# Four layers on one core: other queues, buffers and orders where two layers meet

## The chip, the core and the metric

The kernel runs on one core of a Trainium2 chip. The metric is the device time of one execution in microseconds (us). The kernel before took 2582.68 us in the median of 3 runs (2582.19 to 2583.7).

A core has engines that run beside each other, each with its own list of instructions, worked off in order: TensorE (PE; its weight loads are shown as PEld), VectorE (DVE), ScalarE (ACT), GpSimd (POOL) and SyncE (SP), which here only issues DMAs. An instruction that waits for a semaphore holds up everything behind it on its engine.

## The reference, cut to what matters

Two kinds of layer follow each other, A, B, A, B, each with a layer norm before it and a residual around it. x is 2048 x 640, both kinds have 32 heads. A has heads of 20 and four segments of 512 tokens; B has heads of 128, 64 segments of 32 tokens, and 8 memory rows that each segment passes on to the next.

```python
def _A_ref(x, wq, wk, wv, wo, beta):           # Dh = 20, N = 4, L = 512
    ...
    for s in range(N):
        qs, ks, vs = (q[:, :, s].copy(), k[:, :, s].copy(), v[:, :, s].copy())
        p = _softmax(jnp.einsum('bhqd,bhkd->bhqk', qs, ks) * scale + mask, axis=-1)
        a_dot = jnp.einsum('bhqk,bhkd->bhqd', p, vs)
        pq = phi(qs)
        num = jnp.einsum('bhld,bhde->bhle', pq, M)
        den = jnp.einsum('bhld,bhd->bhl', pq, z)[..., None] + 1e-06
        outs.append(g * num / den + (1.0 - g) * a_dot)
        pk = phi(ks)
        M = M + jnp.einsum('bhld,bhle->bhde', pk, vs)
        z = z + jnp.einsum('bhld->bhd', pk)
    return concat(outs) @ wo

def _B_ref(x, mem0, Wq, Wk, Wv, Wo, seg_len):  # Dh = 128, 64 segments of 32, M = 8
    ...
    mem = mem0
    for s in range(n_seg):
        h = jnp.concatenate([mem, xs], axis=1)  # 40 rows
        q, k, v = (jnp.einsum('btd,dhe->bhte', h, W) for W in (Wq, Wk, Wv))
        p = _softmax(where(mask, jnp.einsum('bhqe,bhke->bhqk', q, k) * scale, -1e9))
        o = jnp.einsum('bhte,hed->btd', jnp.einsum('bhqk,bhke->bhqe', p, v), Wo)
        mem = o[:, :M, :].copy()
        outs.append(o[:, M:, :])
    return jnp.concatenate(outs, axis=1)

x = x + _A_ref(_layernorm(x), ...)
x = x + _B_ref(_layernorm(x), ...)
x = x + _A_ref(_layernorm(x), ...)
x = x + _B_ref(_layernorm(x), ...)
```

The memory rows of the last segment (the 8 rows of `mem` after s = 63) are not part of the output.

## The kernel before, in words

**Layer A** (line 251 on) works on a segment of four tiles of 128 tokens. `seg_norm` loads a tile (a_xt), takes its statistics on DVE (a_ln_st, a_ln_mv, a_ln_rstd) and makes the normed tile a_xn; `seg_tr` transposes it on PE (a_tps) and ACT or DVE copies it to a_xnT. `proj_q` and `proj_kv` make a_QP, a_KV and from them a_qT, a_KVt, a_kT. Then, for group after group, come scores (a_S), their exponentials (a_PT) and the rest. At the end of a segment `out_stage_b` (line 366 on) multiplies by wo (a_YP), adds the residual (a_xr, loaded here; line 372) on DVE to a_xnew, stores it (line 386), copies it to bf16 (a_xnb, line 389) and stores that as well (xres_bf, line 392). B's layer norm reads xres_bf. In the last segment the copy is ACT's. a_xnb is one buffer. `unread` (a_W) puts matmuls on PE whose result nobody reads.

**Layer B** (line 789 on) first does the things that have no recurrence: it loads b_wv (five chunks of 1 MB, line 776) and b_wo (eight chunks, line 780), norms the first rows (b_xt, b_lntps, b_HX, b_TX), and projects the last 8 tokens of 16 segments at a time: `tail_unit` (b_tail; 16 units of 20 matmuls: Q and K by 8 groups of heads), evacuated by `tail_evac` to b_tu (eight places, DVE and ACT by turns) and stored to b_QKd by SP (line 952). `vtail_unit` (b_vtail) does the same for V. Then come 64 steps. A step projects its 32 rows (8 of memory, 24 of the segment): Ka, Qa, Kb, Qb (halves of the heads, 20 matmuls each), transposes (b_TPak and so on), scores (b_SP), softmax, V (b_Va, b_Vb), P times V (b_OTP), copies to b_OTsb, output projection b_OPS with b_wo, and from that the next memory rows (b_msb, b_MT). The last 8 tokens of a segment are query rows one step later; so output rows come as 24 rows of one segment (b_XO, `store_head`) and 8 rows of the segment before. The latter are collected in b_OTdef over four steps and multiplied four steps later in chunks (`od_chunk`, b_OPSd, b_XOd, `tail_dma`). Step 63 is followed by nothing: the last collected rows (b_XOe) get a b_OPSd of their own behind it.

**What sets the order.** All PE instructions, and in layer B those of ACT, DVE and POOL too, are chained in the order of the program text (`_OrdNC`, line 120). Layer A's other engines are ordered by a key, `K.base` plus a lag for the kind of instruction. SP's DMAs are put in order by the tile scheduler. A DMA signals on one of eight semaphores in turn, and waits for the DMA eight before it. The pools of A and B lie over each other in SBUF: b_wv's 40 KB per partition cover the places of A's weights and of the pools pxT (a_xnT), pxt (a_xt) and pxn (a_xn). A tile waits for the last readers of what lay in its place (`reuse_waits="tile"`).

**A's weights** come padded: the first A layer stores a_wq_pad and a_wkv to DRAM, the second loads them from there in `load_A_weights` (lines 231 to 233), all by SP.

Of the kernel before, what the change touches and what calls it, by code (L numbers as in the profile page):

```python
# [28 lines left out]
D = 640  # L29
# [27 lines left out]
def build_consts(nc, tc, C):  # L57
    with ExitStack() as tctx:
        tp_ = tctx.enter_context(tc.tile_pool(name="consts_tmp", bufs=1))
        ones = tp_.tile([128, 128], F32, name="c_ones")  # L60
        nc.vector.memset(ones[:], 1.0)
        identf = tp_.tile([128, 128], F32, name="c_identf")
        nc.gpsimd.affine_select(out=identf[:], in_=ones[:], pattern=[[-1, 128]], compare_op=ALU.is_equal,
                                fill=0.0, base=0, channel_multiplier=1)
        nc.vector.tensor_copy(C.identb[:], identf[:])
        nc.vector.memset(C.mhalf[:], -0.5)
        negs = tp_.tile([128, 128], F32, name="c_negs")
        nc.vector.memset(negs[:], -1e9)
        neguf = tp_.tile([128, 128], F32, name="c_neguf")
        nc.gpsimd.affine_select(out=neguf[:], in_=negs[:], pattern=[[1, 128]], compare_op=ALU.is_gt,  # L70
                                fill=0.0, base=0, channel_multiplier=-1)
        for i in range(2):
            nc.vector.tensor_copy(C.negu[:, i, :], neguf[:])
        nc.vector.memset(C.pad[:], 0.0)
        nc.vector.memset(C.pad[:, 0, 0:2], 1.0)
        nc.vector.memset(C.pad[:, 1, 0:1], 1.0)
        nc.vector.memset(C.bdmask[:], 0.0)
        for j in range(4):
            nc.vector.memset(C.bdmask[32 * j:32 * j + 32, 32 * j:32 * j + 32], 1.0)
# [143 lines left out]

def load_A_weights(nc, W, A_wq, A_wk, A_wv, A_wo, padded, stage):

    first = not padded
    if first:
        for nm, src in (("wq", A_wq), ("wk", A_wk), ("wv", A_wv)):
            nc.sync.dma_start(stage[nm], src.rearrange("(c p) n -> p c n", p=128))
    else:  # L230
        nc.sync.dma_start(W.wq[:].rearrange("p c h s -> p (c h s)"), padded["wq"])
        nc.sync.dma_start(W.wkv[:].rearrange("p c g n -> p (c g n)"), padded["wkv"])
# [17 lines left out]
def layer_A(nc, tc, C, W, x_src, x_dst, src_is_bf16, nseg=4, out_bf16=False, xb_dst=None, load_w=None, side_loads=None):  # L250
# [7 lines left out]
    with ExitStack() as ctx:  # L258
# [69 lines left out]
        def seg_norm(n_, tt):  # L328
# [4 lines left out]
            for i in range(2):  # L333
                K("st").vector.bn_stats(out=stats[:, i, :], in_=xt[:, 320 * i:320 * i + 320])
            mv = sml.tile([128, nc.vector.BN_AGGR_DIM], F32, name="a_ln_mv", tag="ln_mv")
# [30 lines left out]
        def out_stage_b(n_, tt, halves=(0, 1)):  # L366
            d = SEG[n_]
            oT, xr = d["oT"][tt], d["xr"][tt]
            r0 = n_ * 512 + tt * 128
            if xr is None:  # L370
                xr = wkl.tile([128, D], BF16 if src_is_bf16 else F32, name="a_xr")
                nc.sync.dma_start(xr[:], x_src[r0:r0 + 128, :])
            if n_ == nseg - 1 and (tt or not src_is_bf16):
# [12 lines left out]
            nc.sync.dma_start(x_dst[r0:r0 + 128, :], xnew[:])  # L386
            xnb = w1l.tile([128, D], BF16, name="a_xnb")
            if n_ == nseg - 1:
# [227 lines left out]
        for tt in range(4):  # L616
            K.base = 0.1 * tt - 100.0
            seg_norm(0, tt)
            K.base = None
            unread((14 if src_is_bf16 else 6, 4, 4, 4)[tt])  # L620
            seg_tr(0, tt)
# [65 lines left out]
        def last_turns(c0, c1):  # L687
            d = SEG[nseg - 1]
            for tt in range(4):
                if c0 == 0:  # L690
                    if tt % 2 == 0:
                        d["tps"] = d.get("tps", []) + [psx.tile([128, 2, 2 * 512], BF16, name="a_otps", tag="x")]
                    xr = wkl.tile([128, D], BF16 if src_is_bf16 else F32, name="a_xr") if tt < 2 else None
                    if tt < 2:
                        nc.sync.dma_start(xr[:], x_src[512 * nseg - 512 + 128 * tt:512 * nseg - 384 + 128 * tt, :])
                    d["xr"][tt] = xr
                tps = d["tps"][tt // 2][:, tt % 2, 0:D].rearrange("p (c t) -> p c t", t=128)
                for c in range(c0, c1):
                    nc.tensor.transpose(tps[:, c, :], d["Onat"][:, tt, 128 * c:128 * c + 128], C.identb[:])
# [89 lines left out]
def layer_B(nc, tc, C, W, x_src, xb_src, x_dst, mem0, B_Wv, B_Wo, nsteps=64, out_bf16=False, tag=""):  # L789
# [8 lines left out]
    with ExitStack() as ctx:  # L798
# [252 lines left out]
        def x_out(ops_, XO_, store, nm):  # L1051
            nc.vector.tensor_tensor(out=XO_[:], in0=ops_[0:64, :], in1=XO_[:], op=ALU.add)
            if out_bf16:
                xo = wk.tile([64, 320], BF16, name=f"b_xnb{nm}", tag=f"xnb{nm}")
            else:
# [4 lines left out]
        def store_head(s):  # L1060
            def f(xo):
                for jj2 in range(2):
                    nc.sync.dma_start(d_half(x_dst[32 * s:32 * s + 24, :], jj2), xo[32 * jj2:32 * jj2 + 24, :].rearrange("t (c x) -> t c x", x=64))
            return f

        def tail_dma(s0, store, xo):
            x_ = x_dst if store else x_src
            for jj2 in range(2):
                sb = xo[32 * jj2:32 * jj2 + 32, :].rearrange("t (c x) -> t c x", x=64)
                dr = x_[32 * s0:32 * s0 + 128, :].rearrange("(i t) (c j x) -> i t j c x", t=32, j=2, x=64)[:, 24:32, jj2]  # L1070
                if store:
# [16 lines left out]

        def od_end():
            x_out(od["ps"], od["xo"], lambda xo: tail_dma(od["s0"], True, xo), "d")  # L1090
            od.clear()
# [8 lines left out]
        for s in range(nsteps):  # L1100
# [11 lines left out]
            for jj2 in range(2):  # L1112
                nc.sync.dma_start(XO[32 * jj2:32 * jj2 + 24, :].rearrange("t (c x) -> t c x", x=64), d_half(x_src[32 * s:32 * s + 24, :], jj2))

# [61 lines left out]
            ka = kq(Ka, "act")  # L1176
            Qa = thin_mm(cols, W.wq, 0, "b_Qa")
            qa = kq(Qa, "dve", SCB)
            Kb = thin_mm(cols, W.wk, 1, "b_Kb")
            kb = kq(Kb, "act")  # L1180
            Qb = thin_mm(cols, W.wq, 1, "b_Qb")
            qb = kq(Qb, "act", SCB)
# [4 lines left out]
            TPaq = transp4(qa, "b_TPaq")  # L1187
            scatter("dve", TPaq, 0, QT[s], 0, 8, 24)
            x_scatter(TPaq, 0, QT)
# [4 lines left out]
            TPbq = transp4(qb, "b_TPbq", po.tile([128, 4, 128], BF16, name="b_TPbq", tag="tail"))  # L1194
            scatter("dve", TPbq, 1, QT[s], 0, 8, 24)
            x_scatter(TPbq, 1, QT)
            SPb = mask_mm(1)
# [25 lines left out]
            if unit:  # L1223
                tail_evac(unit[0], unit[1], "act")
            otf = [ps_tile([128, 2, 4, 40] if j else [128, 4, 40], F32, "b_OTP") for j in range(4)]
            ots = {j: (otf[j][:, 0, :, :], otf[j][:, 1, :, :]) for j in (1, 2, 3)}
# [50 lines left out]
            if od and od["n"] == 4:  # L1277
                od_end()
                if last:
                    od_begin(s - 3, XOe, "tail")  # L1280
                else:
                    tail_dma(s - 3, False, XOd)
                    od_begin(s - 3, XOd)
            elif s == 3:
# [5 lines left out]
            x_out(ops, XO, store_head(s), "")  # L1290
            nc.gpsimd.tensor_copy(OTdef[(s // 4) % 2][:, :, 8 * (s % 4):8 * (s % 4) + 8], OTsb[:].rearrange("p (h c) -> p h c", c=40)[:, :, 0:8])
            if ln_due(s + 1):
                ln_load(ln_due(s + 1))
            QT.pop(s, None); KT.pop(s, None); VH.pop(s - 1, None)
        for _ in range(4):
            od_chunk()
        od_end()


def full_kernel(tc, A_x, A_wq, A_wk, A_wv, A_wo, A_beta, B_x, B_mem0, B_Wq, B_Wk, B_Wv, B_Wo, B_seg_len, out, layers="ABAB"):  # L1300
    nc = tc.nc
    with ExitStack() as ctx:
# [13 lines left out]
        for li, L in enumerate(layers):  # L1316
            lastl = (li == nl - 1)
            if L == "A":
                first = li == 0

                def side(slot, after):
                    if slot % 3 == 1 and slot // 3 < 8 * NCH:
                        load_B_resident(nc, WB, B_Wq, B_Wk, slot // 3, after)
                    if slot == 24:
                        keep_padded(nc, tc, WA, padded)

                layer_A(nc, tc, C, WA, xin if first else X, X, first, xb_dst=Xb,
                        load_w=lambda: load_A_weights(nc, WA, A_wq, A_wk, A_wv, A_wo, padded, stage),
                        side_loads=(side, A_beta) if first else None)
# [60 lines left out]
```

## Time and profile before

| what | us |
|---|---|
| median of 3 runs | 2582.68 |
| profiled execution, its time | 2584.32 |
| its span | 2582.6 |
| PE busy | 2502.8 (97%) |
| DVE busy | 1642.7 (64%) |
| ACT busy | 1513.3 (59%) |
| POOL busy | 658.7 (26%) |
| DMA queue of the kernel | 148.26 MB, 22.0% of 16 engines |

The mean granted clock is 0.995. In the profile's 40 slices PE is in its ninth tenth nearly everywhere; the slices around the joints (slice 5 of layer A to B, 20 of B to A, 25 and 26 of A to B) are where DVE and ACT change their load.

How to read what follows: in a timeline a row is start, duration, engine, line, operation, out<-in by the program's names, count, and in brackets how long the engine stood idle before it and what ended that. Line 110 and line 139 are the helpers that record every operation of an ordered engine, so one goes by the names of tiles. In the list of waits a row is who waits for whom, us in total, how often, the longest. SPq is SP issuing a DMA: its duration is that of the issue, not of the transfer.

### The profile page before, as it was taken

The page shows a single profiled execution, that of the slowest core. Times are in us where ns is not written, and L with a number is a line of the kernel's source. Part 1 is how long each engine was busy: PE and PEld are TensorE (multiplying, and loading weights), DVE is VectorE, ACT ScalarE, POOL GpSimd, SP SyncE. Part 2 cuts the span into 40 slices and gives each one's busy share as a digit, 9 for nine tenths or more (in the row PEclk, how much of TensorE's full clock was granted, in tenths as well). Part 3 has the DMA queues.
Part 4 walks back from the last instruction along what each step waited for, and adds up shares of the span by engine and source line. Part 5 has one row for each costly group of instructions (what it writes and reads, how often), then busy time and mean ns, then how long its engine had stood idle before and what let it go on. Part 6 is the DMA issues. An engine that isn't in the chain of part 4 may idle for free.

```text
span 2582.6 us, 142252 instructions
## 1 busy us (share of the span) xinstructions
PE 2502.8 (97%) x63624; PEld 1646.8 (64%) x63624; DVE 1642.7 (64%) x4599; ACT 1513.3 (59%) x3302; POOL 658.7 (26%) x1431
## 2 busy tenths in 40 slices
PE   8999989999999999999989999999999999999998
PEld 5566666666666666666655666766666666666665
DVE  8888745556556555555678887555655555565555
ACT  6898845555555555454469888455555555555443
POOL 5576621111111111111135665211111111111110
PEclk9999999999999999999989999999999999999999
DMA  4122272222222222111120112712112122211111
GB/s 158 46 82 79 77 249 47 48 47 45 44 51 48 46 50 45 39 36 34 50 97 18 64 53 59 260 44 48 44 41 48 41 46 45 44 42 34 38 26 21
DMA packets 325317, 157.35 MB, mean 61 GB/s; under 512 B 244960, under 2 KB 309600, under 8 KB 322912
## 3 DMA queue, kind: packets, MB, share of 16 engines
q1 hardware_dynamic: 324704, 148.26, 22.0%
q8 instruction: 497, 8.14, 1.3%
q14 instruction: 116, 0.95, 0.1%
HBM read 96.46 MB, written 51.71 MB: 57 GB/s over the span
## 4 chain that ended last, share of the span: by engine, by line
PE 83%; DVE 8%; ACT 6%; issue 1%; DMA 1%; POOL 0%; SPq 0%; ACTq 0%; DVEq 0%
PE b_OPS L110 11%; PE b_tail L110 6%; PE b_Ka L110 5%; PE b_Qb L110 5%; PE b_Kb L110 5%; PE b_Qa L110 5%; PE b_Va L110 4%; PE b_SP L110 4%; PE b_Vb L110 4%; PE a_S L110 4%; ACT a_PT L139 3%; PE b_vtail L110 3%; PE b_OPSd L110 3%; DVE a_nm L139 3%; PE b_OTP L110 3%; PE a_QP L110 2%
## 5 line engine op out<-in xcount | busy, mean ns | idle before, releaser
L110 PEld LDWEIGHTS <-b_HX 128*32 128x32 bf16 x15360 | 428.6, 96 | 330.7 <-DVE b_HX L110 0.7
L139 DVE TENSOR_REDUCE a_nm<-a_S 128x2 f32<-128x512 f32 (+3 forms) x512 | 396.0, 817 | 79.9 <-PE a_S L110 59.4
L110 POOL TENSOR_TENSOR b_Pn<-b_E,b_rs 128x200 bf16<-128x200 bf16 x128 | 78.1, 610 | 1337.7 <-PE b_Vb L110 894.9
L139 ACT ACTIVATE a_PT<-a_T 128x1024 bf16<-128x1024 f32 (+1 forms) x384 | 341.3, 893 | 43.4 <-PE a_T L110 34.9
L110 PE MATMUL b_OPS<-b_wo,b_OTsb 128*32 128x320 bf16 x8192 | 302.2, 299 | 2.2 <-issue 1.2
L110 PEld LDWEIGHTS <-b_OTsb 128*32 128x32 bf16 x8192 | 205.6, 96 | 76.3 <-DVE b_OTsb L110 3.9
L139 POOL TENSOR_SCALAR_AFFINE_SELECT a_PT<-a_PT 128x256 bf16<-128x256 bf16 x380 | 185.5, 493 | 196.7 <-ACT a_PT L139 196.5
L110 DVE CAST b_HX<-b_MT 128x8 bf16<-128x8 f32 x372 | 63.6, 172 | 234.3 <-PE b_MT L110 228.5
L110 ACT CAST b_msb<-b_OPS 128x64 bf16<-128x64 f32 x378 | 69.3, 256 | 223.4 <-PE b_OPS L110 223.4
L110 ACT CAST b_kq<-b_Kb 128x512 bf16<-128x512 f32 x128 | 74.9, 585 | 201.6 <-PE b_Kb L110 201.6
L110 DVE COPY b_KT<-b_TPak 128x128 bf16<-128x128 bf16 x128 | 28.7, 224 | 228.2 <-PE b_TPak L110 228.2
L110 DVE TENSOR_SCALAR b_kq<-b_Qa 128x512 bf16<-128x512 f32 x128 | 88.5, 691 | 119.4 <-PE b_Qa L110 116.3
L110 PE MATMUL b_Va<-b_wv,b_HX 128*32 128x512 bf16 x2520 | 161.0, 380 | 0.0
L110 PE MATMUL b_Vb<-b_wv,b_HX 128*32 128x512 bf16 x2520 | 160.7, 379 | 0.0
L110 PEld LDWEIGHTS <-b_kq 128*128 128x128 bf16 x2080 | 116.8, 98 | 68.6 <-ACT b_kq L110 55.2
L110 PE MATMUL b_Kb<-b_wk,b_HX 128*32 128x512 bf16 x2520 | 158.2, 379 | 0.0
L110 PE MATMUL b_Qb<-b_wq,b_HX 128*32 128x512 bf16 x2520 | 158.2, 379 | 0.0
L110 PE MATMUL b_Qa<-b_wq,b_HX 128*32 128x512 bf16 x2520 | 158.2, 379 | 0.0
L110 PE MATMUL b_Ka<-b_wk,b_HX 128*32 128x512 bf16 x2520 | 158.2, 379 | 0.0
L110 DVE CAST b_OTsb<-b_OTP 128x160 bf16<-128x160 f32 (+1 forms) x384 | 131.0, 376 | 36.1 <-PE b_OTP L110 29.7
L110 ACT CAST b_kq<-b_Ka 128x512 bf16<-128x512 f32 x128 | 74.9, 585 | 108.1 <-PE b_Ka L110 108.1
L110 PE MATMUL b_vtail<-b_wv,b_TX 128*32 128x256 bf16 x2880 | 133.3, 271 | 2.9 <-issue 2.9
(208 smaller groups left out, 5389.3 us busy)
## 6 DMA issues: line engine op xcount, KB each, us to landing
b_QKd<-b_tu SPq DMA_DIRECT2D x128, 128.0 KB
b_tl<-b_QKd SPq DMA_DIRECT2D x64, 256.0 KB
b_wv<-in_B_Wv_dram SPq DMA_DIRECT2D x10, 1024.0 KB
b_wo<-in_B_Wo_dram SPq DMA_DIRECT2D x16, 640.0 KB
b_Vth<-b_VTd SPq DMA_DIRECT2D x512, 16.0 KB
b_XO<-xres SPq DMA_DIRECT2D x256, 30.0 KB
b_VTd<-b_vt SPq DMA_DIRECT2D x224, 32.0 KB
b_xt<-xres_bf SPq DMA_DIRECT2D x40, 160.0 KB
```

Of the source, the lines that this page charges most:

```text
L110: r = f(*a, **k)
L139: r = f(*a, **k)
```

## The change

It has six parts.

1. At the start DVE's first work is tied behind the constants (`after_consts`), and the key of the four norms of the first segment goes from 0.1 per tile to 1.2 per tile, so that a tile's norm is finished before the next begins. This holds in both A layers.
2. The second A layer's a_wkv is loaded by ACT's queue, behind the last ACT instruction of layer B (`act_last`).
3. In the last segment of an A layer the residuals of tiles 2 and 3 are loaded at the same point as those of tiles 0 and 1, into places of the pool pxt (a_xt).
4. There, bf16 copies of tiles 1 and 2 go to places of pxn (a_xn), that of tile 3 to a place of pxT (a_xnb3).
5. The last step of B makes no new queries for rows that come after the end: Qa, Qb and their transposes and copies are gone; QT's 8 columns are set to zero. Its output rows are all taken from b_OPS (columns 0 to 32 of b_OTsb in place of 8 to 40).
6. The remaining b_OPSd chunks (one of the running four, and four of b_XOe with three segments) go ahead of b_OTP, and their additions and stores ahead of those of b_XO.

```diff
@@ constants
-            nc.vector.tensor_copy(C.negu[:, i, :], neguf[:])
+            C.after_consts = nc.vector.tensor_copy(C.negu[:, i, :], neguf[:])
@@ load_A_weights
-        nc.sync.dma_start(W.wkv[:].rearrange("p c g n -> p (c g n)"), padded["wkv"])
+        f = nc.scalar.dma_start(W.wkv[:].rearrange("p c g n -> p (c g n)"), padded["wkv"])
+        tc.add_manual_dep(f.ins, C.act_last.name, mybir.DependencyInfo(mybir.DependencyClass.NoSync, mybir.DependencyReason.SCHED_ONLY), reason="order")
@@ seg_norm
-                K("st").vector.bn_stats(out=stats[:, i, :], in_=xt[:, 320 * i:320 * i + 320])
+                f = K("st").vector.bn_stats(out=stats[:, i, :], in_=xt[:, 320 * i:320 * i + 320])
+                if src_is_bf16 and n_ + tt + i == 0:
+                    tc.add_manual_dep(f.ins, C.after_consts.ins.name, K.info, reason="order")
@@ out_stage_b
-            if xr is None:
-                xr = wkl.tile([128, D], BF16 if src_is_bf16 else F32, name="a_xr")
-                nc.sync.dma_start(xr[:], x_src[r0:r0 + 128, :])
...
-            xnb = w1l.tile([128, D], BF16, name="a_xnb")
+            if n_ == nseg - 1 and tt in (1, 2):
+                xnb = pxn.tile([128, D], BF16, name="a_xn")
+            elif n_ == nseg - 1 and tt == 3:
+                xnb = pxT.tile([128, D], BF16, name="a_xnb3", tag="xnT")
+            else:
+                xnb = w1l.tile([128, D], BF16, name="a_xnb")
@@ layer_A, first segment
-            K.base = 0.1 * tt - 100.0
+            K.base = 1.2 * tt - 100.0
@@ last_turns
-                    xr = wkl.tile([128, D], BF16 if src_is_bf16 else F32, name="a_xr") if tt < 2 else None
-                    if tt < 2:
-                        nc.sync.dma_start(xr[:], x_src[512 * nseg - 512 + 128 * tt:512 * nseg - 384 + 128 * tt, :])
+                    dt_ = BF16 if src_is_bf16 else F32
+                    xr = wkl.tile([128, D], dt_, name="a_xr") if tt < 2 else pxt.tile([128, 2 * D] if src_is_bf16 else [128, D], dt_, name="a_xt")
+                    nc.sync.dma_start(xr[:, 0:D], x_src[512 * nseg - 512 + 128 * tt:512 * nseg - 384 + 128 * tt, :])
@@ layer_B, a step
-            Qa = thin_mm(cols, W.wq, 0, "b_Qa")
-            qa = kq(Qa, "dve", SCB)
+            if last:
+                nc.gpsimd.memset(QT[s][:, :, 24:32], 0.0)
+            else:
+                Qa = thin_mm(cols, W.wq, 0, "b_Qa")
+                qa = kq(Qa, "dve", SCB)
...
+            if last:
+                od_chunk()
+                oda = dict(od)
+                od_begin(s - 3, XOe, "tail")
+                for _ in range(4):
+                    od_chunk()
...
+            if last:
+                od_end(oda)
+                od_end(nm="e")
             od_chunk(0)
...
-                o_mm(ops, lambda h: OTsb[:, 40 * h + 8:40 * h + 40], [16 * a + 4 * j + 2 * ip for ip in range(2)], n_ == 0, n_ == 7)
+                o_mm(ops, lambda h: OTsb[:, 40 * h + 8 - 8 * last:40 * h + 40 - 8 * last], [16 * a + 4 * j + 2 * ip for ip in range(2)], n_ == 0, n_ == 7)
...
-        for _ in range(4):
-            od_chunk()
-        od_end()
+        C.act_last = nc._prox["scalar"]._last
```

Left out above: Qb and the two transposes of the queries stand in the same kind of branch; `store_head` and the load of b_XO move 24 and 8 rows apart in the last step; `tail_dma` takes three segments for b_XOe; b_XOe's bf16 result has a buffer of its own.

More of the change, by code (lines that the diff above doesn't have):

```diff
@@ L221, in build_gates, with load_A_weights @@
     nc.vector.tensor_copy(W.go[:, 0:2, 1, :], W.omg[:, 24:32].rearrange("p (G j) -> p G j", j=4))
-def load_A_weights(nc, W, A_wq, A_wk, A_wv, A_wo, padded, stage):
+def load_A_weights(nc, tc, C, W, A_wq, A_wk, A_wv, A_wo, padded, stage):
     first = not padded
@@ L1053, in x_out @@
             if out_bf16:
-                xo = wk.tile([64, 320], BF16, name=f"b_xnb{nm}", tag=f"xnb{nm}")
+                xo = (bx if nm == "e" else wk).tile([64, 320], BF16, name=f"b_xnb{nm}", tag="tl" if nm == "e" else f"xnb{nm}")
             else:
@@ L1062, in f @@
                 for jj2 in range(2):
-                    nc.sync.dma_start(d_half(x_dst[32 * s:32 * s + 24, :], jj2), xo[32 * jj2:32 * jj2 + 24, :].rearrange("t (c x) -> t c x", x=64))
+                    for r0, t0, t1 in (((0, 0, 24),) if s < nsteps - 1 else ((8, 0, 24), (0, 24, 32))):
+                        r_ = 32 * jj2 + r0
+                        nc.sync.dma_start(d_half(x_dst[32 * s + t0:32 * s + t1, :], jj2), xo[r_:r_ + t1 - t0, :].rearrange("t (c x) -> t c x", x=64))
             return f
@@ L1067, in tail_dma @@
             x_ = x_dst if store else x_src
+            n_ = min(4, nsteps - 1 - s0) if store else 4
             for jj2 in range(2):
-                sb = xo[32 * jj2:32 * jj2 + 32, :].rearrange("t (c x) -> t c x", x=64)
-                dr = x_[32 * s0:32 * s0 + 128, :].rearrange("(i t) (c j x) -> i t j c x", t=32, j=2, x=64)[:, 24:32, jj2]
+                sb = xo[32 * jj2:32 * jj2 + 8 * n_, :].rearrange("t (c x) -> t c x", x=64)
+                dr = x_[32 * s0:32 * s0 + 32 * n_, :].rearrange("(i t) (c j x) -> i t j c x", t=32, j=2, x=64)[:, 24:32, jj2]
                 if store:
@@ L1087, in od_chunk, with od_end @@
                     od["n"] = k + 1
-        def od_end():
-            x_out(od["ps"], od["xo"], lambda xo: tail_dma(od["s0"], True, xo), "d")
+        def od_end(od=od, nm="d"):
+            x_out(od["ps"], od["xo"], lambda xo: tail_dma(od["s0"], True, xo), nm)
             od.clear()
@@ L1112, in layer_B @@
             for jj2 in range(2):
-                nc.sync.dma_start(XO[32 * jj2:32 * jj2 + 24, :].rearrange("t (c x) -> t c x", x=64), d_half(x_src[32 * s:32 * s + 24, :], jj2))
+                for r0, t0, t1 in (((0, 0, 24),) if not last else ((0, 24, 32), (8, 0, 24))):
+                    r_ = 32 * jj2 + r0
+                    nc.sync.dma_start(XO[r_:r_ + t1 - t0, :].rearrange("t (c x) -> t c x", x=64), d_half(x_src[32 * s + t0:32 * s + t1, :], jj2))
             def x_scatter(tp, b, D_):
@@ L1176, in layer_B @@
             ka = kq(Ka, "act")
-            Qa = thin_mm(cols, W.wq, 0, "b_Qa")
-            qa = kq(Qa, "dve", SCB)
+            if last:
[3 more added lines that the diff above has]
+                qa = kq(Qa, "dve", SCB)
             Kb = thin_mm(cols, W.wk, 1, "b_Kb")
             kb = kq(Kb, "act")
-            Qb = thin_mm(cols, W.wq, 1, "b_Qb")
-            qb = kq(Qb, "act", SCB)
+            if not last:
+                Qb = thin_mm(cols, W.wq, 1, "b_Qb")
+                qb = kq(Qb, "act", SCB)
             TPak = transp4(ka, "b_TPak")
@@ L1186, in layer_B @@
             x_scatter(TPak, 0, KT)
-            TPaq = transp4(qa, "b_TPaq")
-            scatter("dve", TPaq, 0, QT[s], 0, 8, 24)
-            x_scatter(TPaq, 0, QT)
+            if not last:
+                TPaq = transp4(qa, "b_TPaq")
+                scatter("dve", TPaq, 0, QT[s], 0, 8, 24)
+                x_scatter(TPaq, 0, QT)
             TPbk = transp4(kb, "b_TPbk")
@@ L1193, in layer_B @@
             SPa = mask_mm(0)
-            TPbq = transp4(qb, "b_TPbq", po.tile([128, 4, 128], BF16, name="b_TPbq", tag="tail"))
-            scatter("dve", TPbq, 1, QT[s], 0, 8, 24)
-            x_scatter(TPbq, 1, QT)
+            if not last:
+                TPbq = transp4(qb, "b_TPbq", po.tile([128, 4, 128], BF16, name="b_TPbq", tag="tail"))
+                scatter("dve", TPbq, 1, QT[s], 0, 8, 24)
+                x_scatter(TPbq, 1, QT)
             SPb = mask_mm(1)
@@ L1278, in layer_B @@
                 od_end()
[L1279 to L1283, printed above, removed]
+                tail_dma(s - 3, False, XOd)
+                od_begin(s - 3, XOd)
             elif s == 3:
@@ L1290, in layer_B @@
             x_out(ops, XO, store_head(s), "")
-            nc.gpsimd.tensor_copy(OTdef[(s // 4) % 2][:, :, 8 * (s % 4):8 * (s % 4) + 8], OTsb[:].rearrange("p (h c) -> p h c", c=40)[:, :, 0:8])
+            if not last:
+                nc.gpsimd.tensor_copy(OTdef[(s // 4) % 2][:, :, 8 * (s % 4):8 * (s % 4) + 8], OTsb[:].rearrange("p (h c) -> p h c", c=40)[:, :, 0:8])
             if ln_due(s + 1):
@@ L1327, in full_kernel @@
                 layer_A(nc, tc, C, WA, xin if first else X, X, first, xb_dst=Xb,
-                        load_w=lambda: load_A_weights(nc, WA, A_wq, A_wk, A_wv, A_wo, padded, stage),
+                        load_w=lambda: load_A_weights(nc, tc, C, WA, A_wq, A_wk, A_wv, A_wo, padded, stage),
                         side_loads=(side, A_beta) if first else None)
```

## The prediction

> **What bounds the kernel now.** I read the page first: busy shares and the chain that ended last.
>
> ```profile
> span 2582.6 us, 142252 instructions
> ...
> PE 83%; DVE 8%; ACT 6%; issue 1%; DMA 1%; POOL 0%; SPq 0%; ACTq 0%; DVEq 0%
> ```
>
> TensorE (PE) carries 83% of the chain and is busy 97% of the span, so only PE's gaps can be won. The steady steps of layer B, about 14 us each, 64 in each B layer, keep their instructions. What is left are five places: the start (0 to 20 us), three joints (A to B at 317 to 396, B to A at 1276 to 1312, A to B at 1608 to 1684) and the end (from 2560). I read waits and timeline for each. First the waits in 345 to 374, then PE's timeline there:
>
> ```profile
> ACT a_xnb L389 <- DMA xres_bf<-a_xnb: 3.9, 1, 3.9
> ...
> PE b_tail L110 <- ACT b_tu L110: 2.6, 1, 2.6
> ```
>
> ```profile
> 352.05 4.46 PE L110 MATMUL b_tail<-b_TX,b_wq 128*128 128x128 bf16 x77
> 359.06 4.92 PE L110 MATMUL b_tail<-b_TX,b_wq 128*128 128x128 bf16 x60 [2.55 <-ACT b_tu L110]
> ```
>
> ScalarE (ACT) waits for the store of the one a_xnb buffer; behind that wait stand its evacuations of the tail units (b_tu), and PE stands 2.55 us. In the third joint that gap is 1.3. Next SyncE's (SP) queue in the first joint (stretches 315 to 330 and 348 to 384):
>
> ```profile
> 317.65 0.81 SPq L776 DMA_DIRECT2D b_wv<-in_B_Wv_dram  x2
> ...
> 325.54 1.70 SPq L776 DMA_DIRECT2D b_wv<-in_B_Wv_dram  x2
> ```
>
> ```profile
> 359.05 0.38 SPq L780 DMA_DIRECT2D b_wo<-in_B_Wo_dram  x1
> 359.52 6.58 SPq L952 DMA_DIRECT2D b_QKd<-b_tu  x9
> ```
>
> The five 1 MB loads of b_wv are issued at 317 to 327, long before use, and the first chunk of b_wo just ahead of the b_tu stores. The second joint:
>
> ```profile
> 1298.66 0.50 SPq L232 DMA_DIRECT2D a_wkv<-a_wkv_home  x1
> ...
> 1306.48 2.85 PE L110 MATMUL a_KV<-a_wkv,a_xnT 128*128 128x160 bf16 x20 [5.30 <-DMA a_wkv<-a_wkv_home]
> ```
>
> a_wkv leaves late, behind stores that wait for VectorE (DVE), and PE waits 5.30 us for it.
>
> **The change, part by part.** Orders and waits are those of the two compiled programs; durations are those of the profile.
>
> *Start.* DVE makes c_identb and c_negu first, then norms tile by tile. Now PE waits 8.6 us for c_negu, then the projection of K and V runs 17.15 to 18.84 and the first scores at 20.3. The transposes come earlier, but a_wv lands at 14.32 (DMA completion records) and beta at 17.04, and ACT's gate exponential, which waits for beta, stands ahead of its copy to a_qT. So scores start at about 19.8: **-0.5** (bounds -1.7 if ACT's order doesn't hold, 0 if it holds fully).
>
> *First joint.* Residuals of tiles 2 and 3 are loaded early, and tiles 1 to 3 have bf16 buffers of their own. The wait above goes, with 2.55 us of gap and about 1.6 of slow clock behind it (100 tail matmuls after the gap took 7.15 us against 5.59). But these buffers lie in places that b_wv is laid over. In the changed program the first b_wv load waits for the last stores of these buffers, and on SP all five now stand behind the first b_wo chunk and ahead of every b_tu store. What that costs: PE's a_YP ends at 352.05, DVE adds and the 0.72 us ACT copy follow, the last bf16 store leaves at 353.5, b_wo at 353.9. b_wo took 4.9 us from issue to landing (359.05 to 363.95); b_wv chunks land 2.70 and 2.76 us apart (322.56, 325.26; 333.03, 335.79). So b_wv is complete at 353.9 + 4.9 + 5 x 2.74 = 372.5. A check by rate:
>
> ```profile
> 374.00:383.00 9.00, 8.97 (x240) 6.47 (x232) 3.71 (x9) 3.24 (x7) 0.00 (x0) 1.00 1.08 383
> ```
>
> This stretch (last column GB/s, before it the DMA share) has three b_wo chunks back to back at 383 GB/s; 5.24 MB at that rate is 13.7 us, the same. The b_tu stores now land one after another behind their b_wo chunk: 364.28 after 363.95. So the first lands at 372.8, where it lands at 364.28 today. b_tu has 8 places: evacuation 9 of 16 waits for that landing, PE for the evacuation four units later. PE starts tails at 351, has twelve units done at about 364.8 and stands until 373.2; four units (80 matmuls took 4.63 us) and transposes end at 378.4, against 373.47 now: +4.9. Behind it the profile has a 2.02 us gap "<-issue" at 383.46 and b_V at 4.05 us where the third joint needs 2.26; that is 3.8 us that may or may not recur. I take half: **+3.0** (bounds -4.1, only the gains, to +5.8, a later and colder end).
>
> *Third joint.* The same, and the cover is thinner now already:
>
> ```profile
> 1654.94 0.59 ACT L110 CAST b_tu<-b_tail 128x512 bf16<-128x512 f32 x1 [3.25 <-DMA b_QKd<-b_tu]
> ```
>
> One b_wo chunk ahead of the stores holds ACT 3.25 us here; five b_wv chunks more follow it in the change. Shifted by 1290.76 us tails would end at 1668.6 (the clock stays at 1.00 here) against 1661.61, with no slow stretch behind it to win back: **+7.0** (+4 to +8.4, or -2 if nothing takes the place of the gap). In both joints seven b_wo chunks (1.9 us each) and the first b_tl load come behind the stores, complete at about 392.5; scores need them at 398.
>
> *Second joint.* The last step of B drops Qa and Qb (1.08 each) and two transposes (0.22, 0.30); Kb's evacuation is then uncovered, so I count 1.9 of 2.7. V ends at 1282.8 instead of 1284.69. The 80 deferred output matmuls (0.034 each by the 64 in 2.17 us, so 2.7) move ahead of b_OTP: it starts at 1285.6, as now at 1285.76. What PE wins there it loses to DVE: the norm statistics of tiles 0 and 1 stand ahead of the b_OTsb copies and wait for a_xt, which lands 2.8 us after V's end (1284.71 to 1287.49). With 1.31 us a tile, b_OTsb comes at 1288.7, two more at 1290.2 and 1290.6, b_OPS ends at 1291.9 (now 1289.0). Tile 3's statistics end at 1296.7, a_xn of it at 1297.9, transposes and copy at 1299.0: a_QP at 1299.1, now 1299.94. a_KV then doesn't wait: a_wkv leaves ACT's queue at about 1287.3, and a_wq and a_wkv (2.9 MB) behind 1.3 MB of a_xt land at 1296 by the 383 GB/s. a_KV runs at 1300.4 against 1306.48: **-6** (bounds -7.5, if the DVE order costs nothing, to -4, if transfers share badly).
>
> [...]
>
> *End.* The same -1.9 and the 2.7 us of matmuls ahead of b_OTP; the last rows come out of b_OPS itself, so the 64 matmuls behind it go (2.2 us), and so does this wait for a buffer in the chain:
>
> ```profile
> 2575.60 2.17 DMA out_dram<-b_xnbd
> ```
>
> b_OTP starts at 2569.9 (2570.11 now), b_OPS ends at 2573.2, six adds of 0.49 end at 2574.6. Eight stores at 0.7 us of issue each, from 2572.7, then end at 2578.3 at SP, against 2579.78: **-1.4** (-2.2 to -0.9).
>
> **Sum**: -0.5 + 3.0 - 6 + 7.0 - 1.4 = **+2.1 us**. The profiled execution took 2584.32 us, 1.7 outside its span and 1.64 above the median of 2582.68. The differences are laid on the median: **2584.8**. Bounds of the terms together give -8 to +10.
>
> **Rivals.**
> A, the forecast: 2584.8.
> B, slower: the slow stretch behind the tails comes in both A-to-B joints, because b_wo chunks land under vtail and b_V. It decides if b_wo's last chunk lands after 386, as today in the first joint (386.08); by my working it does (392). Price 3.8 a joint: first +5, third +10.4, sum +7.5: 2590.2. Against it: in the third joint DMAs were as busy (0.95) under b_V, and PE lost only 0.41.
> C, faster: b_tu stores aren't held behind b_wv, or twelve units and what else PE has cover it. Then -4.1 and -2 stand instead of +3 and +7: sum -14, 2568.7. Against it: the 3.25 us of ACT above.
> D, a_wkv doesn't come earlier: sharing with a_wq and a_xt it lands near 1304, the joint gives -2: +6.1, 2588.8. Against it: its 7.8 us from issue to a_KV (1298.66 to 1306.48) had a_wo and four tile loads beside it.
>
> **How the numbers follow.** A 0.43, B 0.25, C 0.17, D 0.15. 0.2% (5.2 us) is about what a measurement of this kernel can tell from no change: faster is below 2577.5, slower above 2587.9. A gives 0.05 / 0.33 / 0.05 to faster, same, slower; B 0 / 0.03 / 0.22; C all its 0.17 to faster; D 0.01 / 0.04 / 0.10. Together 0.23, 0.40, 0.37. The range 2572 to 2594 takes in the terms' bounds, B and D; it leaves out most of C and the end of B, some 0.19. A alone: 2579 to 2590.
>
> **What would show it.** Right: PE standing 6 to 9 us in the tails of both A-to-B joints, b_wv issued right behind b_wo at about 354 and 1645; in the second joint no wait of a_KV, but b_OPS waiting on b_OTsb; at the end no b_OPSd behind b_OPS. Wrong: no gap of PE in the tails (C), a_KV still waiting on a_wkv (D), gaps "<-issue" or a clock under 0.9 behind the tails in the third joint (B).

## The result and the profile after

The changed kernel took 2594.78 us in the median of 6 runs (2592.55 to 2598.88), the kernel before beside it 2583.19 (2581.41 to 2586.2): a ratio of 1.0046, with a 95% interval of 1.0033 to 1.0059. It is slower by some 12 us. The profiled execution has a span of 2592.9 us against 2582.6.

To see where the 10.3 us between the two profiled executions arise, I took the start of the same PE instruction in both timelines, place by place:

| first instruction of | before | after | difference |
|---|---|---|---|
| a_S on a_kT, start | 20.32 | 20.11 | -0.2 |
| last a_PV of the first A layer | 341.51 | 341.57 | +0.1 |
| b_Kp (tails done) | 373.40 | 381.31 | +7.9 |
| first step's b_Ka | 391.43 | 397.69 | +6.3 |
| last step's b_Ka | 1276.07 | 1283.79 | +7.7 |
| b_OPS of that step | 1286.70 | 1296.45 | +9.7 |
| second A layer's first a_KV | 1306.48 | 1307.69 | +1.2 |
| a quarter of its a_PV | 1409.12 | 1408.13 | -1.0 |
| last a_PV | 1632.29 | 1631.30 | -1.0 |
| b_Kp | 1661.54 | 1671.94 | +10.4 |
| first step's b_Ka | 1676.16 | 1687.57 | +11.4 |
| last step's b_Ka | 2560.49 | 2572.62 | +12.1 |
| end of the last instruction | 2582.61 | 2592.93 | +10.3 |

So the first A-to-B joint loses 6.2 us, the B-to-A joint wins 8.7, the other A-to-B joint loses 12.4, the end wins 1.8. The steady steps between drift by 1.5 and 0.7. In the first B layer (425 to 1270) PE's waits of 0.2 us and more add up to 4.1 us instead of 3.1, most of it "<-issue"; I put nothing on that, since the last a_PV of the first A layer differs by 2.0 us (341.51 and 339.55) between single executions of two kernels that are the same up to there.

The page's head and its chain:

```profile
span 2592.9 us, 141993 instructions
...
PE 81%; DVE 8%; ACT 6%; DMA 2%; issue 2%; SPq 0%; POOL 0%; ACTq 0%; DVEq 0%
```

There are fewer instructions, and yet PE has 81% of the chain instead of 83%, and DMA 2% instead of 1%.

PE's timeline of the changed kernel in the first and in the second A-to-B joint:

```profile
362.19 2.40 PE L110 MATMUL b_tail<-b_TX,b_wk 128*128 128x128 bf16 x40
374.54 4.33 PE L110 MATMUL b_tail<-b_TX,b_wk 128*128 128x128 bf16 x40 [9.95 <-ACT b_tu L110]
```

```profile
1651.93 2.40 PE L110 MATMUL b_tail<-b_TX,b_wk 128*128 128x128 bf16 x40
1665.52 3.98 PE L110 MATMUL b_tail<-b_TX,b_wk 128*128 128x128 bf16 x40 [11.20 <-ACT b_tu L110]
```

The gaps of 2.55 and 1.3 us are gone, and gaps of 9.95 and 11.20 us stand in their place, later in the tails. The row behind each gap has the same 40 matmuls as the row ahead of it and takes 4.33 and 3.98 us instead of 2.40. What holds ACT, from the waits of the first of the two joints (345 to 380):

```profile
ACT b_tu L110 <- DMA b_QKd<-b_tu: 14.5, 1, 14.5
POOL b_ln_rstd L110 <- DVE b_ln_rstd L110: 14.3, 4, 5.1
DVE b_tu L110 <- DMA b_QKd<-b_tu: 13.7, 1, 13.7
```

and SP's queue there:

```profile
354.31 0.38 SPq L785 DMA_DIRECT2D b_wo<-in_B_Wo_dram  x1
354.87 2.85 SPq L781 DMA_DIRECT2D b_wv<-in_B_Wv_dram  x5
357.75 20.04 SPq L957 DMA_DIRECT2D b_QKd<-b_tu  x13
```

The loads of b_wv, issued at 317 to 327 before, stand between the first chunk of b_wo and the stores of b_tu. By the DMA completion records b_wo lands at 358.70, the last b_wv chunk at 373.47, the first b_tu store at 373.80. What b_wv waits for shows in the same records: the store of the last bf16 copy lands at 354.66 and the first b_wv is issued at 354.87; in the second A-to-B joint these are 1645.38 and 1645.40. The clock behind the gap, in stretches of 2 us (columns: length, busy time of PE, PEld, DVE, ACT, POOL with counts, PEclk, DMA share, GB/s):

```profile
374.00:376.00 2.00, 1.46 (x15) 1.46 (x15) 1.38 (x2) 1.57 (x3) 0.00 (x0) 0.50 0.55 186
376.00:378.00 2.00, 2.00 (x21) 2.00 (x20) 0.00 (x0) 0.59 (x1) 0.00 (x0) 0.50 0.53 177
378.00:380.00 2.00, 2.00 (x34) 2.00 (x32) 0.69 (x1) 0.56 (x1) 0.00 (x0) 0.84 0.56 115
380.00:382.00 2.00, 2.00 (x41) 1.57 (x42) 0.58 (x1) 0.59 (x1) 0.00 (x0) 1.00 1.10 360
```

PE goes on at half its clock for some 4 us: 15 and 21 matmuls instead of the 41 of the last stretch.

In the B-to-A joint PE's rows are:

```profile
1296.45 0.45 PE L110 MATMUL b_OPS<-b_wo,b_OTsb 128*32 128x320 bf16 x8 [2.94 <-DVE b_OTsb L110]
...
1306.62 1.24 PE L110 MATMUL a_QP<-a_xnT,a_wq_pad 128*128 128x512 bf16 x4 [0.34 <-ACT a_xnT L139]
...
1307.69 0.85 PE L110 MATMUL a_KV<-a_wkv,a_xnT 128*128 128x160 bf16 x10
```

a_KV no longer waits for a_wkv, and b_OPS waits for b_OTsb, which DVE makes only after two tiles of statistics. At the end of the program no b_OPSd stands behind b_OPS.

### The profile page after: what moved, and what is told of

It reads as the page before. It is cut to its first block, busy times and chain, and to the rows that moved or that the text cites. A ratio compares the mean times of both kernels' runs of the same rounds, so it can differ in the third digit from the quotient of the medians.

```text
span 2592.9 us, 141993 instructions
## 1 busy us (share of the span) xinstructions
PE 2494.7 (96%) x63464; PEld 1645.3 (63%) x63528; DVE 1639.1 (63%) x4593; ACT 1512.9 (58%) x3300; POOL 659.0 (25%) x1431
## 4 chain that ended last, share of the span: by engine, by line
PE 81%; DVE 8%; ACT 6%; DMA 2%; issue 2%; SPq 0%; POOL 0%; ACTq 0%; DVEq 0%
PE b_OPS L110 11%; PE b_tail L110 5%; PE b_Ka L110 5%; PE b_Kb L110 5%; PE b_Qa L110 5%; PE b_Qb L110 5%; PE b_Va L110 4%; PE b_Vb L110 4%; PE b_SP L110 4%; PE a_S L110 4%; ACT a_PT L139 3%; PE b_vtail L110 3%; PE b_OPSd L110 3%; DVE a_nm L139 3%; PE b_OTP L110 3%; PE a_T L110 2%
## 5 line engine op out<-in xcount | busy, mean ns | idle before, releaser
L110 DVE COPY b_KT<-b_TPak 128x128 bf16<-128x128 bf16 x128 | 28.8, 225 | 227.2 <-PE b_TPak L110 227.2
```

The source lines that it names most:

```text
L110: r = f(*a, **k)
```

## The experiments

The theory: parts 3 and 4 use places that b_wv is laid over; b_wv is late, and in SP's queue it holds up the b_tu stores. Rivals: the loss comes from the other parts; or it is the amount that has to cross in that stretch, whatever its order. Ratios are to the kernel before on the same chip, in five rounds each. The kernel before took 2584.38, 2580.90 and 2582.41 us on the three chips used here, so the ratios are what can be compared, and not the medians.

| kernel | median us | ratio, 95% interval |
|---|---|---|
| change | 2594.78 | 1.0046 (1.0033 to 1.0059) |
| change without parts 3 and 4 | 2577.78 | 0.9975 (0.9965 to 0.9985) |
| before with parts 3 and 4 alone | 2601.29 | 1.0067 (1.0053 to 1.0080) |
| change with part 4, without 3 | 2604.19 | 1.0084 (1.0071 to 1.0098) |
| change, b_tu stores by ACT's queue | 2584.45 | 1.0004 (0.9994 to 1.0014) |
| change, b_wv between the b_tu stores | 2588.04 | 1.0033 (1.0024 to 1.0043) |
| change, bf16 copies in a_Onat's place | 2575.56 | 0.9967 (0.9954 to 0.9979) |
| the same, statistics behind b_OTsb | 2569.11 | 0.9955 (0.9943 to 0.9968) |
| that one again, on another chip | 2572.1 | 0.9958 (0.9946 to 0.9971) |
| that one with a_wkv on SP's queue | 2571.09 | 0.9956 (0.9944 to 0.9969) |
| before with part 2 alone | 2579.86 | 0.9996 (0.9987 to 1.0005) |
| before with parts 5 and 6 alone | 2579.88 | 0.9994 (0.9986 to 1.0003) |

**Without parts 3 and 4.** The four edits of `out_stage_b` and `last_turns` in the diff above are undone, and nothing else.

> The changed kernel without its parts 3 and 4 (residuals of the last tiles loaded late, one a_xnb buffer, as before). Theory: the loss sits in the two A-to-B joints alone (first b_Ka after them 6.3 and 12.4 us later against the stretch ahead of them, by the traces of before and after), because these buffers make b_wv wait. Then all of it goes: 2594.8 - 18.7 = 2576, with b_wv issued at about 317 to 327 again and PE's gap in the tails back at 2.5 and 1.3 us. Rival: the other parts cause the loss in the joints (other order of DVE and of the queues): 2590 to 2595.

Ratio 0.9975: the loss is gone, and what is left of the change wins 6 us. The first b_Ka behind the joints comes 1.1 and 7.9 us earlier than before, not 6.3 and 11.4 later. The first b_wv is issued at 319.99 again, and the gaps in the tails are 2.34 and 0.63 us. Behind the first of them the 60 matmuls take 3.51 us (granted clock 1.00 from 357 to 364), where they took 4.92 behind the gap of 2.55 us in the kernel before (0.50 from 359 to 361, 0.74 in the next 2 us):

```profile
361.23 3.51 PE L110 MATMUL b_tail<-b_TX,b_wq 128*128 128x128 bf16 x60 [2.34 <-ACT b_tu L110]
```

**Parts 3 and 4 alone**, the same edits on the kernel before.

> The kernel before with parts 3 and 4 alone. Theory: 2583.2 + 18.7 = 2602, PE standing 10 and 11 us in the tails of the A-to-B joints. Rival (the parts only lose together with the others): 2580 to 2585.

1.0067, some 17 us more, with gaps of 10.2 and 9.6 us in the tails; its first b_Ka behind the second A-to-B joint is 16.0 us late. The loss belongs to these parts and needs none of the others. Part 3 alone was not run.

**Part 4 without part 3**: the residuals late again, the copies in their own places.

```diff
+            if xr is None:
+                xr = wkl.tile([128, D], BF16 if src_is_bf16 else F32, name="a_xr")
+                nc.sync.dma_start(xr[:], x_src[r0:r0 + 128, :])
```

> The changed kernel with part 4 alone of the two buffer parts (own bf16 copies in pxn and pxT, residuals of tiles 2 and 3 late). Theory: part 4 by itself makes b_wv wait for the last stores, so nothing of the loss goes: ratio to before 1.004 to 1.006, PE's gap in the tails 9 us or more. Rival: it needs both parts: 0.997 to 0.999.

1.0084, slower than the whole change and than I expected. The waits of PE in the two A-to-B joints are the longest of all kernels:

```profile
PE b_tail L110 <- ACT b_tu L110: 12.9, 1, 12.9
PE b_vtail L110 <- issue: 2.1, 1, 2.1
```

```profile
PE b_tail L110 <- ACT b_tu L110: 12.0, 1, 12.0
PE b_tail L110 <- DVE b_tu L110: 0.8, 1, 0.8
```

So the copies alone make b_wv wait, and the early residuals take some of it back: with them the last store, and so b_wv, leaves earlier (the first b_wv at 354.87 in the change, at 359.02 here).

**The stores on another queue.** Everything of the change stays, and b_wv is late; the sixteen stores are issued by ACT.

```diff
-            tail_evac(0, k, "act" if k % 2 == 0 else "dve", tu_homes[k % 8])
+            tail_evac(0, k, "act" if k % 2 == 0 else "dve", tu_homes[k % 8], nc.scalar.dma_start)
```

> The changed kernel with the sixteen b_tu stores of each layer start issued by ACT's queue in place of SP's; b_wv stays late. Theory A (order in SP's queue: the stores stand behind 5.2 MB of b_wv): the stores land within 3 us, PE's gap shrinks from 10 and 11 us to under 3, and the time to 2576 to 2582. Theory B (the DMA engines are full, whichever queue a store comes from): the stores share 380 GB/s with b_wv and b_wo, the gap stays above 7 us and the time at 2591 to 2596.

1.0004, above the times of theory A, and PE's gap in the tails is not small but gone. The timeline of the first joint shows the units in one go:

```profile
353.05 9.10 PE L110 MATMUL b_tail<-b_TX,b_wq 128*128 128x128 bf16 x160
361.99 2.40 PE L110 MATMUL b_tail<-b_TX,b_wk 128*128 128x128 bf16 x40
364.50 4.63 PE L110 MATMUL b_tail<-b_TX,b_wk 128*128 128x128 bf16 x80
369.25 2.40 PE L110 MATMUL b_tail<-b_TX,b_wk 128*128 128x128 bf16 x40
```

But this edit changes more than the queue of the stores. SP's timeline shows that the loads of b_wv are spread out too:

```profile
357.21 14.98 SPq L781 DMA_DIRECT2D b_wv<-in_B_Wv_dram  x5
```

In the change the five loads are issued within 2.85 us, ahead of every store. Here the stores stand between them in the turn of the eight semaphores, and each DMA waits for the one eight before it (in the change SP's stores wait 11.9 us for loads of b_wv in this way, five times, 3.1 at the longest). So the loads are issued at 357.21, 361.26, 364.24, 368.98 and 371.87, two stores leave ahead of the first of them, and two loads are under way at once (three for 0.4 us). By the completion records the stores of the first joint land 2.3 to 9.3 us after they are issued, not within the 3 us of theory A; one that ACT issued 0.23 us behind a load of b_wv landed 0.20 us behind it (376.75 and 376.55). What the run shows is that the same bytes in another order leave no gap in the tails, which theory B excluded. Whether a store on ACT's queue would get past five loads under way on SP's is not shown.

And 7 us against the kernel without parts 3 and 4 remain. In the second joint 46.7 us pass from the last a_PV to the first b_Ka, without parts 3 and 4 43.0; PE now waits there for evacuations:

```profile
PE b_Kp L110 <- ACT b_tu L110: 1.3, 1, 1.3
PE b_TP L110 <- DVE b_kq L110: 1.2, 1, 1.2
```

ACT stands between its evacuations until a DMA of its own can be issued (in the first joint 3.25 us ahead of b_kq, for a load of b_wv). In the first step PE also waits for a load that SP issues late:

```profile
PE b_OTP L110 <- DMA b_Vth<-b_VTd: 1.0, 2, 0.5
```

From the first step's b_Ka to the third's it takes 30.8 us, without parts 3 and 4 27.7; in the other joint it is 31.1 against 28.9. Together that is 9.0 of the 9.9 us between the profiled executions of the two kernels.

**b_wv between the stores.** The call `load_B_wv(nc, W, B_Wv)` moved behind the loop over the sixteen tail units; same bytes, same buffers.

> The changed kernel with the call that loads b_wv moved behind the sixteen tail units in the text, so that SP's list has the five b_wv loads between the b_tu stores and not all ahead of them; same bytes, same buffers, b_wv still late. Theory A (order in SP's queue): PE's gap in the tails falls from 10 and 11 us to under 3, and the time to 2578 to 2586; what is left against the kernel without parts 3 and 4 (2578) is that 5.2 MB more cross ahead of the first step's b_tl and b_Vth, as in the kernel with b_tu on ACT's queue, where PE waits 1.0 us for b_Vth. Theory B (too many bytes in that stretch): gaps above 7 us, 2591 to 2596.

1.0033. The 2588.04 us lie between the two theories' times, but the kernel before was faster on this chip, and by the ratio the time is at the lower end of theory B's; the gaps in the tails are as theory A has them. The trace says why: the tails have no gap, but V's units wait (waits of PE in the first joint and the first steps):

```profile
PE b_vtail L110 <- DMA b_wv<-in_B_Wv_dram: 6.6, 3, 3.2
PE a_otps L110 <- DVE a_Onat L139: 0.6, 1, 0.6
PE b_OTP L110 <- DMA b_Vth<-b_VTd: 0.4, 1, 0.4
```

Behind the last of these waits 144 matmuls of b_vtail take 7.17 us (granted clock 0.55 from 382 to 391); in the change 154 of them take 4.43 (1.00 from 386 to 392).

```profile
384.60 7.17 PE L110 MATMUL b_vtail<-b_wv,b_TX 128*32 128x256 bf16 x144 [2.21 <-DMA b_wv<-in_B_Wv_dram]
```

In these runs the order in the queue settles which consumer pays (9.95 us at b_tail in the change, 6.6 at b_vtail here), and the lateness of b_wv that one of them does. Theory A had looked for what is left in the first step's b_tl and b_Vth; b_wv's own reader pays most of it.

**The copies elsewhere.** Without part 3, and with the copies in a place of a_Onat's pool that the segment before has left:

```diff
-            xnb = w1l.tile([128, D], BF16, name="a_xnb")
+            if n_ == nseg - 1 and tt:
+                if tt == 1:
+                    d["xnb4"] = pon.tile([128, 4, D], BF16, name="a_xnb4", tag="Onat")
+                xnb = d["xnb4"][:, tt, :]
+            else:
+                xnb = w1l.tile([128, D], BF16, name="a_xnb")
```

> The changed kernel with the residuals loaded late as before, but with the bf16 copies of the last tiles 1 to 3 in a free place of the pool of a_Onat, which b_wv isn't laid over. Theory: b_wv is early, the wait of ACT for the store of the one buffer is gone too: PE's gaps of 2.55 and 1.3 us in the tails and the slow clock behind them (1.6 us) go, so 3 to 5 us under the kernel without these parts: 2571 to 2573. Rival (ACT then waits for the late residuals, and the gaps only change their name): 2575 to 2577, as without parts 3 and 4.

0.9967 against 0.9975: in the right direction, but the intervals overlap, so that the 3 to 5 us I expected aren't shown by the times, and 2575.56 us is in the rival's range. I had taken the gaps and the slow clock from the kernel before; in the kernel to compare with, the gaps were 2.34 and 0.63 us and the clock behind them wasn't slow (1.00 from 357 to 364 and from 1641 to 1648), so that less than 3 us was there to win. In the trace PE no longer waits for ACT in the tails; from the last a_PV to b_Kp it takes 2.5 us less than without these parts in the first joint (27.8 against 30.3), and nothing less in the second (28.8 against 28.6), where PE waits 0.80 us for DVE's b_tu in place of 0.63 for ACT's.

**Statistics behind b_OTsb.** To the kernel above, one line that ties the second A layer's first statistics to the last b_OTsb copy of DVE.

```diff
+            C.last_ot = nc._prox["vector"]._last
...
+                if not src_is_bf16 and n_ + tt + i == 0:
+                    tc.add_manual_dep(f.ins, C.last_ot.name, K.info, reason="order")
```

> The kernel with the bf16 copies in a_Onat's place (2575.6), and the second A layer's first statistics tied behind the last b_OTsb copy of DVE. Theory: b_OPS no longer waits 3.6 us, but DVE's norms set the end of the joint, and DVE wins only the time in which it waited for a_xt: 0 to 1.5 us less, 2574 to 2576. Rival: b_OPS is what sets the joint: 3 us less, 2572.5.

> The same kernel as before this one, for a comparison on the same chip: ratio to before 0.9955 (0.994 to 0.997).

0.9955, and 0.9958 on another chip: the fastest kernel of this study, 10 to 12 us under the kernel before. Against the kernel above it is 3 us, more than my theory had and what the rival had, though the intervals overlap. In its trace b_OPS doesn't wait; a_KV starts 14.9 us after b_OTP (1280.61 to 1295.47), in the kernel above 16.1.

**Part 2 alone.**

> The kernel before with part 2 alone: a_wkv by ACT's queue. Theory: PE's wait of 5.3 us for a_wkv goes, since on SP it stood behind stores that wait for DVE: 2584 - 5 = 2579. Rival D: the transfer shares the engines with a_wq and a_xt and lands as late as before: 2582 to 2585.

0.9996: no difference that can be told, as rival D said (in the one trace the joint wins 3.4 us, in the times of 12 runs 1.0 with an interval that holds zero). The wait of 5.3 us for a_wkv is gone, and one of 6.69 stands ahead of it (before, 3.12). DVE's timeline shows from where:

```profile
1292.66 0.89 DVE L139 BATCH_NORM_STATS2 a_ln_st<-a_xt 128x6 f32<-128x320 f32 x2 [2.45 <-DMA a_xt<-xres]
...
1295.36 0.49 DVE L139 BATCH_NORM_STATS2 a_ln_st<-a_xt 128x6 f32<-128x320 f32 x1 [1.39 <-DMA a_xt<-xres]
```

```profile
1298.38 1.46 PE L110 MATMUL a_W<-c_negu,c_identb 128*128 128x256 bf16 x6 [6.69 <-DVE a_ln_rstd L139]
```

a_wkv was issued at 1286.90, 2.0 us behind the first a_xt, and the tiles 2 and 3 of a_xt, which wait 0.2 us at most in the kernel before, wait 2.45 and 1.39. The stretch 1290 to 1295 moves 407 GB/s, before 276. What a_wkv won, a_xt lost.

**Parts 5 and 6 alone**: `layer_B` of the change in the kernel before.

> The kernel before with parts 5 and 6 alone (last step without new queries, deferred matmuls ahead of b_OTP). Theory: in the B-to-A joint the 2 us that PE wins ahead of b_OTP are lost again, since statistics of the next norm that wait for a_xt come ahead of the b_OTsb copies on DVE (b_OPS waits 3 to 4 us), and a_wkv is late as before, so nothing there; at the end 1.8 us: 2582 to 2583. Rival: both ends keep their 2 us and the 2.2 us of matmuls behind: 2577 to 2579.

0.9994, as expected. b_OPS waits 4.2 us for b_OTsb, a_KV 4.1 for a_wkv.

**a_wkv back on SP's queue**, in the fastest kernel.

> The fastest kernel so far (copies in a_Onat's place, first statistics behind b_OTsb) with a_wkv back on SP's queue. Alone on the kernel before, part 2 had given nothing that could be told, because a_xt landed later. Theory: here a_xt is issued 2 us earlier against a_wkv and the norms are no longer late, so SP's order decides: PE waits about 4 us for a_wkv, the ratio to before goes from 0.9955 to 0.997. Rival: part 2 gives nothing here either: 0.995 to 0.996.

0.9956 beside 0.9958: nothing, the rival was right, and my reason was wrong. SP's timeline shows what I had not thought of:

```profile
1280.91 0.43 SPq L231 DMA_DIRECT2D a_wq_pad<-a_wq_home  x1
1281.38 0.43 SPq L232 DMA_DIRECT2D a_wkv<-a_wkv_home  x1
...
1283.79 1.51 SPq L1084 DMA_DIRECT2D xres<-b_XOd  x2
```

The scheduler put a_wkv ahead of the stores by itself here; with parts 5 and 6 alone it is issued at 1292.89, behind them. Whether part 1 or the tie of DVE's statistics makes the difference wasn't tried. In this kernel it isn't the engine that issues the load that counts, but what stands ahead of it.

## Why the prediction was wrong

The forecast was 2584.8, the range 2572 to 2594; it came to 2594.78. The orders and waits came as worked out. The step that failed is the price of the gaps in the two A-to-B joints: the matmuls behind a gap were taken at full clock, and the transfers that end the gap were taken too short. The first of these could have been read from the prediction's own rows. It counts 1.6 us of slow clock behind the gap of 2.55 us in the kernel before as a gain, and then prices the four units behind its own gap of 8.4 us at 4.63 us, which is full clock (1.00 under these 80 matmuls in the kernel before).

- *Start*: -0.5 forecast. First scores 0.2 earlier, and at the end of the layer nothing of it left (+0.1).
- *First A-to-B joint*: +3.0 forecast, +6.2 measured. **This is one of the two terms that failed.** b_wv did stand ahead of the b_tu stores, and the gap came where it was placed (PE stops at 364.6, forecast 364.8). But the first store landed at 373.80, not 372.8; PE went on at 374.54, not 373.2; and the four units behind it began at half the clock, which cost 1.9 us in the first 40 matmuls alone (4.33 against 2.40; the granted clock was 0.50 from 374.5 to about 378.5). In the kernel before, the gap of 2.55 us had the half clock behind it too (0.50 from 359 to 361). Tails ended 7.9 us late, not 4.9. Of the 3.8 us slow stretch behind, of which half was taken to recur, the gap "<-issue" came again (2.05, before 2.02) and the slow b_V didn't (2.36 us to the next instruction, before 4.05; the granted clock was 0.50 from 386 to 388 in the kernel before, and 1.00 here).
- *Second A-to-B joint*: +7.0 forecast, with +8.4 as the upper bound, +12.4 measured. **This is the other, and the larger miss.** The prediction said that the clock stays at 1.00 here. It read that from the stretch before, in which PE stood 1.3 us; with a gap of 11.20 us the clock was halved as in the other joint (0.50 from 1666 to 1668; 40 matmuls in 3.98 us). That is 1.6 us. PE stopped where the forecast had it (23.0 us behind the last a_PV, forecast 23.3), but went on 2.5 us later than forecast: the store of the last bf16 copy landed 14.1 us behind the last a_PV (first joint 13.1), and the five loads of b_wv landed 3.28 us apart, not 2.74 (first joint 2.79). Why they were slower here is open. Ahead of the first b_Ka a gap "<-issue" of 1.40 us stands where one of 0.41 was before. And 0.6 us is a slip of the working: the first joint's 378.4 shifted by 1290.76 us is 1669.2, not 1668.6, so that the term should have been +7.6 and the sum +2.7.
- *B-to-A joint*: -6 forecast, -6.5 measured at a_KV and -8.7 by a quarter of the layer. b_OPS waited for DVE and a_KV no longer for a_wkv, as worked out. The 2.2 us behind a_KV are the clock again, left out with the other sign: behind the gap of 5.30 us in the kernel before it was 0.50 from 1306 to 1314, and 20 matmuls of a_KV took 2.85 us; in the change they take twice 0.85 (clock 1.00 from 1306 to 1310). That this made good a part of the misses in the other joints is luck. The reason given for the -6 was only half right: alone, part 2 can't be told from nothing (0.9996), parts 5 and 6 can't either (0.9994; in the trace they win 1.3 us up to a_KV and nothing by the middle of the layer), and with part 1 together they win 6 us (0.9975 without the buffers). My reading, which no run by itself shows, is that part 2 pays where a_wkv's place among SP's DMAs is late and a_xt is ahead of it; in the fastest kernel, where SP's place is early, it pays nothing. What part 1 has to do with it was not tried by itself.
- *End*: -1.4 forecast, -1.8 measured.

Rival B had the sign, at 2590.2, but by another mechanism: slow stretches behind the tails. Of it only the gaps "<-issue" were there, and in the first joint they are in every profile but one (1.66 to 2.73 us), with and without the change; the one without has b_vtail waiting for b_wv there. C, that the stores aren't held, is refuted by the waits of 14.5 us on them. D is not what happened in the change: a_wkv landed at 1304.79, 11.1 us after its issue and 2.9 us ahead of a_KV. D's -2 for the joint was an estimate that no run shows; the joint gave -6.5 at a_KV in the change, and with part 2 alone nothing that can be told, where a_xt landed late instead of a_wkv.

A smaller fault of the working is in the range: the bounds of the terms, simply added up, are -17.5 and +9.3, not -8 and +10, and in both A-to-B joints the same miss, the clock behind a long gap, was left out of them.

## What to carry to other kernels

A buffer that is put into a "free" place is paid for by whoever is laid over that place next (here b_wv, first issued at 354.87 instead of 317.65): look up what that tile's first writer is, and what is queued behind it on its engine. The late load cost PE here either by what it pushed back in the queue (9.95 us at b_tail) or, moved behind that, by the wait of its own reader (6.6 us at b_vtail): count both. When a forecast puts a gap of several us into TensorE, the matmuls behind the gap belong to the price too (40 of them in 4.33 us instead of 2.40 behind 9.95 us), and so they do when a gap is taken away (20 in 1.70 us instead of 2.85, without the gap of 5.30). And moving a DMA to another engine can move more than that DMA, where the DMAs of both engines wait for each other by turns: with the b_tu stores on ACT's queue, SP issued the five loads of b_wv over 14.98 us instead of 2.85.

## What the hardware showed that I had not expected

- Behind the gap of 9.95 us the granted clock was 0.50 for 4 us and 0.84 in the next 2; behind the gap of 2.55 us in the kernel before it was 0.50 and 0.74 in the stretches 359 to 361 and 361 to 363 as well, and 1.00 behind that. A gap of 1.3 us in the other joint left it at 1.00. The length of the gap alone doesn't decide: at the same place a gap of 2.68 us, in the kernel with part 2 alone, left it at 1.00 too.

```profile
359.20 3.51 PE L110 MATMUL b_tail<-b_TX,b_wq 128*128 128x128 bf16 x60 [2.68 <-ACT b_tu L110]
```

- A 128 KB store issued by SP behind five loads of 1 MB landed 16.0 us after its issue, 0.33 us behind the last of the loads. With the stores issued by ACT and the loads one by one between them, the stores landed 2.3 to 9.3 us after their issue.
- A 1.6 MB load issued by ACT, 1.2 and 0.7 us behind two tile loads of SP, held these up: DVE waited 2.45 and 1.39 us for them, before 0.2 at most.
